# Delta-rule attention and hash-routed experts: the second expert's weights loaded after the last rows, the first expert's last column planned with the attention

## The chip, the core and the metric

The kernel runs on one NeuronCore of a Trainium2 chip. Its engines work side by side, each through its own stream of instructions: TensorE (PE; its weight loads are shown as PEld), VectorE (DVE), ScalarE (ACT), GpSimd (POOL) and SyncE (SP). In this kernel SP issues nearly all transfers, in program order, and POOL issues the scatters of rows. The metric is the device time of one execution in microseconds (us); the kernel before takes 522.31 us, the median of three runs (517.66, 522.31 and 524.82).

## The reference

A delta-rule attention of 4 batches, 8 heads, 768 tokens and a head size of 48 feeds a mixture of 8 experts. A hash of the token's id picks one expert for each token.

```python
k_n = k / (np.linalg.norm(k, axis=-1, keepdims=True) + 1e-06)
for t in range(S):
    y[:, :, t] = np.einsum('bhd,bhde->bhe', q[:, :, t], state)
    v_old = np.einsum('bhde,bhd->bhe', state, kt)
    state = state + bt[:, :, :, None] * np.einsum('bhd,bhe->bhde', kt, vt - v_old)
...
expert_idx = token_ids * np.int64(2654435761) % np.int64(E)
for e in range(E):
    mask = expert_idx == e
    h = np.maximum(xe @ w1[e], 0.0)
    out[mask] = h @ w2[e]
```

The bridge makes 3072 rows of 384 numbers out of the attention's answer. w1 is 384 x 1024 and w2 is 1024 x 384 for each expert, all in float32.

## The kernel before

**Attention.** The 768 tokens are cut into 24 chunks of 32. A chunk asks the state for its values and its answers (`ask`, L631, into psX and psY), solves for its updates (`solve`, L681), adds them to the state (`update`, L704, into psS; the new state is copied out at L727 by ACT and L729 by DVE) and completes the answer (`answer`, L744). The last four chunks (`split`, from `TAIL`) do this in halves, with psX and z1. When a chunk is done, ACT writes its answer to x_sb (L753), and POOL scatters 128 rows to the scratch x_dram, sorted by expert (`store`, L759). DVE computes the triangular inverses and the routing beside it.

**The order** of this part is not written out by hand. Each piece of work is a `task` with an engine, a planned duration, the names it reads and writes, and for matmuls a PSUM bank (`new_job`, `bank`); `order()` plays all tasks through by their planned times and fixes the order on each engine. Tasks marked `idle=True, boost=-1e5` fill PE's idle time or come after the attention. `homes` lists the eight PSUM banks: two z, psX, psY and four psS.

**Experts.** Experts stand in the order `RANKS = [4, 0, 1, 2, 3, 5, 6, 7]`, numbered by how many rows they have. Number 4 is the first expert, number 0 the second, number 1 the third. Each has its own number of rows (up to 424). `gemm1` (L1158) makes the hidden layer in 8 blocks of 128, with the relu on ACT (L1161) and DVE (L1163) in turn; `gemm2_turned` (L1195) or `gemm2` (L1174) gives the result. `send` turns results back (L1205), `store` copies them (L1180), and POOL scatters them to the output (`send_rows`, L1184).

**The first expert** is worked on ahead. Its weights are loaded during the attention into space that is free by then (`weights`, L93 and L959). 18 of the 24 chunks (`SOON`) are enough to hold its first 256 rows (`SC = 2` columns of 128). `early_rows` fetches them to xq0, DVE transposes them (`turn_x`, L107), and `first_expert` adds tasks for both matmuls (L995 and L1006), with the relu at L1000 and the result copied at L1011. Its third column can hold rows of the last chunks. It comes after the attention: `fetch(FIRST)` loads it to xq_late, `turn` transposes it, and `gemm1` and `gemm2` do 128 rows in the first pass of the loop over `RANKS`, in the phase of the experts.

**The second expert's weights** are cut into 8 parts of 384 KB (`load_w_parts`: four of w1 at L93, four of w2 at L124). SP issues three parts after each of the stores that follow the last inverse, so between the last chunks. The third expert's weights are asked for in the first pass of the loop (`between`, `to = i + 2`); x_dram rows of the second are fetched behind those of xq_late, with xq1 as their target.

**PSUM.** The attention's pool `ps` closes at the end of the attention, and three pools open for the experts: `ps_h` with 4 banks for hidden blocks, `ps_t` with 2 for turned results, `ps_o` with 2 for outputs.

## Time and profile before

| what | us |
|---|---|
| the profiled execution's own time | 521.84 |
| its span in the trace | 520.2 |
| median of three runs | 522.31 |
| PE busy in the span | 472.5 (91%) |
| DVE busy | 230.9 (44%) |
| ACT busy | 189.5 (36%) |
| POOL busy | 70.2 (13%) |
| last matmul of the attention ends, by PE's timeline | 247.03 |
| PE begins the second expert | 280.18 |
| last copy of a result begins | 508.18 |

The page gives the busy time of each engine, a picture of the span in 40 slices of 13 us, the queues of the DMA, and the costliest groups of instructions. PEclk is the clock that was granted to PE, in tenths of the full one. In lists of work a line reads: start, duration, engine, line of the kernel, operation, output from input, shapes, how many, and in brackets how long the engine stood idle before and what ended it. "issue" there is idle time in which the engine waited for nothing that the profile shows. SPq is SP's own queue of issued transfers. Large matmuls of float32 leave two records each. A table of stretches gives, for each, the busy time of every engine with its number of records, the granted clock, the DMA's share of busy time (it can go a little above 1) and the rate in GB/s.

### The profile page before, as it was taken

Reading aid. Unit: us, or ns where it says so; the run is one execution under the profiler, and the core shown is the slowest. Engines: PE = TensorE matmul, PEld = TensorE weight load, DVE = VectorE, ACT = ScalarE, POOL = GpSimd, SP = SyncE. Lnnn points to the kernel's source line nnn. Section 1 sums busy time; section 2 is a strip of 40 time slices with the busy share of each in tenths; the row PEclk is TensorE's granted clock in tenths of the full one; section 3 lists DMA queues with packets and bytes.
Section 4 is the critical chain, followed back from the end, with each engine's and each line's share of the span. In section 5 each row is a group of like instructions: output and inputs, shape, how many; then the busy total and the mean of one; then the engine's idle time right before and its main releaser. Section 6 shows DMA issues by size and latency. Waiting matters only on the chain. (4 is left out here: it accounts for less than half of the span.)

```text
span 520.2 us, 15841 instructions
## 1 busy us (share of the span) xinstructions
PE 472.5 (91%) x6652; PEld 322.1 (62%) x6652; DVE 230.9 (44%) x736; ACT 189.5 (36%) x415; POOL 70.2 (13%) x106
## 2 busy tenths in 40 slices
PE   8865999899998888879989999999999999999990
PEld 6654667676776666768766555556555565655650
DVE  5786899899897888643012202103012020120100
ACT  4633687888787677513111101101011020110100
POOL 6000011201102021101010001302202012102010
PEclk9977799999999989968999999999999999999996
DMA  9969758564566274690399954544843006401000
GB/s 145 167 99 139 140 106 148 123 127 90 141 148 129 64 196 92 143 228 34 85 249 203 235 117 129 113 98 137 185 149 82 0 24 159 150 0 41 3 29 15
DMA packets 136748, 60.61 MB, mean 117 GB/s; under 512 B 122957, under 2 KB 131265, under 8 KB 136676
## 3 DMA queue, kind: packets, MB, share of 16 engines
q1 hardware_dynamic: 131140, 49.80, 47.6%
q0 software_dynamic: 5344, 9.66, 5.8%
q8 instruction: 53, 0.87, 0.7%
q10 hardware_dynamic: 192, 0.12, 0.2%
q14 instruction: 19, 0.16, 0.1%
HBM read 49.19 MB, written 10.42 MB: 115 GB/s over the span
## 5 line engine op out<-in xcount | busy, mean ns | idle before, releaser
L1158 PE MATMUL h_ps<-xT,w_sb 128*128 128x424 f32 (+3 forms) x336 | 113.4, 491 | 0.0
L1158 PEld LDWEIGHTS h_ps<-xT,w_sb 128*128 128x128 f32 x336 | 62.9, 190 | 43.1 <-issue 14.9
L1163 DVE TENSOR_SCALAR h_sb<-h_ps 128x424 f32<-128x424 f32 (+4 forms) x32 | 17.0, 531 | 138.7 <-PE h_ps L1158 102.8
L1195 PE MATMUL oT_ps<-h_sb,w_sb 128*128 128x424 f32 (+1 forms) x192 | 66.4, 506 | 0.0
L596 DVE TENSOR_TENSOR tmp<-U,Ni 128x112 f32<-128x112 f32 (+15 forms) x186 | 61.6, 338 | 2.8 <-ACT U L580 0.2
L594 DVE TENSOR_TENSOR U<-U,tmp 128x112 f32<-128x112 f32 (+15 forms) x186 | 61.5, 337 | 2.9
L1184 POOL DMA_INDIRECT out_dram<-o_sb,tokens x26 | 30.3, 1167 | 208.0 <-ACT o_sb L1180 163.0
L1195 PEld LDWEIGHTS oT_ps<-h_sb,w_sb 128*128 128x128 f32 x192 | 36.2, 190 | 28.4 <-issue 15.6
L759 POOL DMA_INDIRECT x_scratch<-x_sb,slot x24 | 24.3, 1011 | 207.5 <-ACT MT L522 123.5
L727 ACT ACTIVATE S<-psS 48x384 f32<-48x384 f32 (+1 forms) x92 | 42.7, 465 | 14.8 <-PE psS L704 13.4
L1174 PE MATMUL o_ps<-w_sb,h_sb 128*121 128x384 f32 (+1 forms) x144 | 46.9, 486 | 0.0
L1161 ACT ACTIVATE h_sb<-h_ps 128x424 f32<-128x424 f32 (+4 forms) x32 | 15.0, 469 | 72.5 <-PE h_ps L1158 72.5
L1174 PEld LDWEIGHTS o_ps<-w_sb,h_sb 128*121 128x121 f32 (+1 forms) x144 | 26.6, 185 | 19.4
L744 PEld LDWEIGHTS psY<-W,MT 64*64 64x64 f32 x768 | 27.0, 144 | 14.0 <-issue 12.4
L704 PE MATMUL psS<-W,K 32*128 32x96 f32 x736 | 28.6, 288 | 5.4 <-ACT W L696 4.7
L744 PE MATMUL psY<-W,MT 64*64 64x48 f32 x768 | 30.8, 230 | 3.0 <-issue 3.0
L1180 ACT COPY o_sb<-o_ps 106x384 f32<-106x384 f32 (+4 forms) x15 | 7.2, 479 | 69.5 <-PE o_ps L1174 55.1
L681 PE MATMUL psX<-R,Tz 64*64 64x48 f32 x672 | 27.9, 223 | 3.5 <-issue 2.5
L704 PEld LDWEIGHTS psS<-W,K 32*128 32x128 f32 x736 | 24.3, 191 | 9.4 <-ACT W L696 7.1
L1197 ACT COPY oT<-oT_ps 128x424 f32<-128x424 f32 (+1 forms) x8 | 4.0, 499 | 70.9 <-PE oT_ps L1195 70.9
L681 PEld LDWEIGHTS psX<-R,Tz 64*64 64x64 f32 x672 | 23.6, 136 | 8.5 <-issue 5.3
L522 ACT ACTIVATE Tz<-TU,kmask 128x256 f32<-128x256 f32 x40 | 25.0, 724 | 0.5 <-DVE TU L610 0.5
(192 smaller groups left out, 586.2 us busy)
## 6 DMA issues: line engine op xcount, KB each, us to landing
w_sb<-in_moe_w_dram SPq DMA_DIRECT2D x32, 384.0 KB
w_sb<-in_moe_w_dram SPq DMA_DIRECT2D x6, 1536.0 KB
keys<-in_k_dram SPq DMA_DIRECT2D x24, 192.0 KB
Qt<-in_q_dram SPq DMA_DIRECT2D x24, 192.0 KB
V<-in_v_dram SPq DMA_DIRECT2D x96, 48.0 KB
K<-in_k_dram SPq DMA_DIRECT2D x96, 48.0 KB
wide<-in_moe_w_dram SPq DMA_DIRECT2D x8, 384.0 KB
xq<-x_scratch SPq DMA_DIRECT2D x12, 144.0 KB
```

Source lines behind the costliest of these rows:

```text
L522: lambda e=e: nc.scalar.activation(out[:, :, e].rearrange(order_of), in_.rearrange(order_of), ACT.Copy, scale=kmask[:, e:e + 1]))
L594: nc.vector.tensor_tensor(U[:, n:, 0:n], U[:, n:, 0:n], t, op=ALU.add)
L596: nc.vector.tensor_tensor(t, U[:, j:n, 0:n].to_broadcast([P, m, n]), Ni[:, j, n:, None].to_broadcast([P, m, n]), op=ALU.mult)
L681: nc.tensor.matmul(pws[i][rows, h], lhsT=Tz[rows, h].rearrange("p e i -> p (e i)"), rhs=R[rows, h], start=(h == (hs.start if split else 0) ...
L704: nc.tensor.matmul(psS[:, b, 2 * D * u:2 * D * u + 2 * D], lhsT=K4[quarter(b), u].rearrange("p r d -> p (r d)"), rhs=W[quarter(b), 2 * u:2 ...
L727: copy = nc.scalar.activation(put, get, ACT.Copy)
L744: nc.tensor.matmul(py[rows, h], lhsT=MT[rows, h].rearrange("p e i -> p (e i)"), rhs=W[rows, h], start=(c == 0 and h == 0), stop=True, skip ...
L759: put = nc.gpsimd.indirect_dma_start(out=x_dram[0:N, :], out_offset=bass.IndirectOffsetOnAxis(ap=slot[:, c:c + 1], axis=0), in_=x_sb, in_o ...
L1158: nc.tensor.matmul(h_ps[:, :width], lhsT=w1_sb[:, co, fo * P:(fo + 1) * P], rhs=xT[:, co, :width], start=(co == 0), stop=(co == CO - 1))
L1174: nc.tensor.matmul(o_ps[0:rows], lhsT=h_sb[:, fo, col * rows:(col + 1) * rows], rhs=w2_sb[:, fo, :], start=(fo == 0), stop=(fo == FO - 1))
L1184: scat = nc.gpsimd.indirect_dma_start(out=out[:, :], out_offset=bass.IndirectOffsetOnAxis(ap=idx, axis=0), in_=rows, in_offset=None, bound ...
L1195: nc.tensor.matmul(oT_ps[:, 0:width], lhsT=w2_sb[:, fo, i * P:(i + 1) * P], rhs=h_sb[:, fo, 0:width], start=(fo == 0), stop=(fo == FO - 1))
```

## The change

Three things are done.

1. The parts of the second expert's weights are no longer issued between the last stores. They follow on SP behind the rows of the late column and the rows of the second expert; the third expert's weights and rows follow them.
2. The first expert's last column becomes a set of tasks, planned with the others. `early_rows` and `number_of` are made general for this (`rows_of`, `columns`). Its input xT_late and its result share a new tile `late`; its hidden layer is kept in xq0; all its relus are ACT's. The loop over `RANKS` skips the first expert.
3. The pool `ps` stays open for the whole program. `hidden()` gives the four banks z0, z1, psX and psY in turn to hidden blocks, and `results()` the four of psS to turned results and outputs alike. xq1 moves from the first pool to a pool of the expert phase, `m_q`.

```diff
-    xqs = [keep.tile([P, NBL, QW], F32, name=f"xq{i}") for i in range(2)]
+    xqs = [keep.tile([P, NBL, QW], F32, name="xq0")]
     xq_late = keep.tile([P, P // C, QW], F32, name="xq_late")
+    late = keep.tile([P, DIN], F32, name="late")
...
+    xT_late, o_late = late.rearrange("p (co x) -> p co x", co=CO), late
+    h_late = xqs[0].rearrange("p i x -> p (i x)")[:, 0:F].rearrange("p (fo x) -> p fo x", fo=FO)
...
-        ps = phase1.enter_context(tc.tile_pool(name="ps", bufs=1, space=PSUM))
+        ps = ctx.enter_context(tc.tile_pool(name="ps", bufs=1, space=PSUM))
...
+            def rows_of(at, cols, xq, numbers):
+                row = value(at, mybir.EngineType.SP, N)
+                got = load_x(row, cols * P // C, xq, nc.sync)
+                got.append(load_numbers(row, cols, P, numbers[:, :, None], nc.sync))
...
+            def columns(name, at, ks, chunks, xq, xq_name, xT):
+                n = ks.stop - ks.start
+                task("SP", 2500, ("x_pad", "lim", *(f"x_dram{i}" for i in range(chunks))),
+                     (xq_name, "numbers" + name),
+                     lambda: rows_of(at, n, xq, numbers_first[:, ks]), kb=200 * n)
+                for c in range(CO):
+                    task("DVE", 70 + 130 * n, (xq_name,), (f"xT{name}{c}",),
+                         lambda c=c: turn_x(xq, n * P // C, xT, c))
+                task("DVE", 220, ("numbers" + name, "lim"), ("idx" + name,),
+                     lambda: number_of(ks))
+
+            columns("", AT_ROW + E + 1, slice(0, SC), SOON, xqs[0], "xq0", xT_first)
...
+            columns("late", AT_ROW + E, slice(SC, SC + 1), NU, xq_late, "xq_late", xT_late)
+            for fo in range(FO):
+                job = new_job(1, early=True)
+                for co in range(CO):
+                    task("PE", 240, ("w1", f"xTlate{co}"), (f"j{job}",),
...
+                         words=2, job=(job, 0), idle=True, boost=-1e5)
+                task("ACT", 290, (f"j{job}",), ("xq0", f"hlate{fo}"), lambda fo=fo, job=job:
+                     nc.scalar.activation(h_late[:, fo], bank(job)[:, 0:P], ACT.Relu),
+                     job=(job, 0))
+            job = new_job(1, early=True)
+            for fo in range(FO):
+                task("PE", 660, ("w2", f"hlate{fo}"), (f"j{job}",),
...
+            task("ACT", 490, (f"j{job}",), tuple(f"xTlate{c}" for c in range(CO)), lambda job=job:
+                 nc.scalar.activation(o_late, bank(job)[:, 0:DIN], ACT.Copy), job=(job, 0))
...
-                if i in stores and parts:
-                    for part in parts[:3]:
-                        part()
-                    parts = parts[3:]
-            for part in parts:
-                part()
-            w_tiles[0] = w1_first, w2_first
...
-         tc.tile_pool(name="m_t", bufs=2) as m_t, \
-         tc.tile_pool(name="ps_h", bufs=4, space=PSUM) as ps_h, \
-         tc.tile_pool(name="ps_t", bufs=2, space=PSUM) as ps_t, \
-         tc.tile_pool(name="ps_o", bufs=2, space=PSUM) as ps_o:
+         tc.tile_pool(name="m_q", bufs=1) as m_q, \
+         tc.tile_pool(name="m_t", bufs=2) as m_t:
+
+        xqs.append(m_q.tile([P, NBL, QW], F32, name="xq1"))
+        banks = itertools.count(), itertools.count()
+
+        def hidden():
+            return homes[next(banks[0]) % 4]
+
+        def results():
+            return homes[4 + next(banks[1]) % 4]
...
         with tc.manual_schedule():
-            fetch(FIRST)
             fetch(RANKS[1])
+            for part in parts:
+                part()
+            w_tiles[2] = load_w(expert_at(RANKS[2], mybir.EngineType.SP), w_pool2, nc.sync)
+            fetch(RANKS[2])
             n_ov = nc.values_load(ov_i[0:1, NOV:NOV + 1], min_val=0, max_val=NOV)
             for c in range(CO):
-                turn(FIRST, c)
+                turn(RANKS[1], c)
             for k in range(SC):
                 send_rows(o_first[:, k], idx_i[:, k:k + 1], True)
+            send_rows(o_late, idx_i[:, SC:SC + 1], True)
             for i, e in enumerate(RANKS):
+                if e == FIRST:
+                    continue
...
-                    to = i + 2 if i < 2 else i + 1
+                    to = max(3, i + 1)
```

More of the change, by code (lines that the diff above doesn't have):

```diff
@@ L140 @@
     h_first = keys.rearrange("p (fo x) -> p fo x", fo=FO)
-    idx_i = keep.tile([P, SC], I32)
-    numbers_first = wide[1][:, FO * DIN + SC * DIN:FO * DIN + SC * DIN + SC]
+    xT_late, o_late = late.rearrange("p (co x) -> p co x", co=CO), late
+    h_late = xqs[0].rearrange("p i x -> p (i x)")[:, 0:F].rearrange("p (fo x) -> p fo x", fo=FO)
+    idx_i = keep.tile([P, SC + 1], I32)
+    numbers_first = wide[1][:, FO * DIN + SC * DIN:FO * DIN + SC * DIN + SC + 1]
     with ExitStack() as phase1:
@@ L970, in first_expert, with number_of @@
                 out=rows, in_=xqs[0].rearrange("p i x -> p (i x)")), kb=700, hold=120000)
-            def early_rows():
-                row = value(AT_ROW + E + 1, mybir.EngineType.SP, N)
-                got = load_x(row, SC * P // C, xqs[0], nc.sync)
-                got.append(load_numbers(row, SC, P, numbers_first[:, :, None], nc.sync))
+            def rows_of(at, cols, xq, numbers):
+                row = value(at, mybir.EngineType.SP, N)
+                got = load_x(row, cols * P // C, xq, nc.sync)
+                got.append(load_numbers(row, cols, P, numbers[:, :, None], nc.sync))
                 for g in got:
                     tc.add_to_no_dep_group("rows", g.ins)
-            task("SP", 2500, ("x_pad", "lim", *(f"x_dram{i}" for i in range(SOON))),
-                 ("xq0", "numbers"), early_rows, kb=400)
-            for c in range(CO):
-                task("DVE", 330, ("xq0",), (f"xT{c}",),
-                     lambda c=c: turn_x(xqs[0], SC * P // C, xT_first, c))
-            def number_of():
-                nc.vector.tensor_tensor(numbers_first, numbers_first,
-                                        none_f[:, FIRST * KT:FIRST * KT + SC], op=ALU.max)
-                nc.vector.tensor_copy(idx_i, numbers_first)
-            task("DVE", 220, ("numbers", "lim"), ("idx",), number_of)
+            def number_of(ks):
+                f = numbers_first[:, ks]
+                nc.vector.tensor_tensor(f, f, none_f[:, FIRST * KT:FIRST * KT + KT][:, ks],
+                                        op=ALU.max)
+                nc.vector.tensor_copy(idx_i[:, ks], f)
+            def columns(name, at, ks, chunks, xq, xq_name, xT):
[9 more added lines that the diff above has]
+            columns("", AT_ROW + E + 1, slice(0, SC), SOON, xqs[0], "xq0", xT_first)
             for fo in range(FO):
@@ L1012, in first_expert @@
                      job=(job, 0))
+            columns("late", AT_ROW + E, slice(SC, SC + 1), NU, xq_late, "xq_late", xT_late)
[3 more added lines that the diff above has]
+                    task("PE", 240, ("w1", f"xTlate{co}"), (f"j{job}",),
+                         lambda fo=fo, co=co, job=job: nc.tensor.matmul(
+                             bank(job)[:, 0:P], lhsT=w1_first[:, co, fo * P:(fo + 1) * P],
+                             rhs=xT_late[:, co], start=(co == 0), stop=(co == CO - 1)),
+                         words=2, job=(job, 0), idle=True, boost=-1e5)
[5 more added lines that the diff above has]
+                task("PE", 660, ("w2", f"hlate{fo}"), (f"j{job}",),
+                     lambda fo=fo, job=job: nc.tensor.matmul(
+                         bank(job)[:, 0:DIN], lhsT=h_late[:, fo], rhs=w2_first[:, fo],
+                         start=(fo == 0), stop=(fo == FO - 1)),
+                     words=2, job=(job, 0), idle=True, boost=-1e5)
+            task("ACT", 490, (f"j{job}",), tuple(f"xTlate{c}" for c in range(CO)), lambda job=job:
+                 nc.scalar.activation(o_late, bank(job)[:, 0:DIN], ACT.Copy), job=(job, 0))
         def note():
@@ L1155, in gemm1 @@
             for fo in range(FO):
-                h_ps = ps_h.tile([P, CAP], F32, name="h_ps")
+                h_ps = hidden()
                 for co in range(CO):
@@ L1171, in gemm2 @@
         def gemm2(w2_sb, h_sb, col, rows, idx, alone):
-            o_ps = ps_o.tile([P, DIN], F32, name="o_ps")
+            o_ps = results()
             for fo in range(FO):
-                nc.tensor.matmul(o_ps[0:rows], lhsT=h_sb[:, fo, col * rows:(col + 1) * rows],
+                nc.tensor.matmul(o_ps[0:rows, 0:DIN], lhsT=h_sb[:, fo, col * rows:(col + 1) * rows],
                                  rhs=w2_sb[:, fo, :], start=(fo == 0), stop=(fo == FO - 1))
@@ L1179, in store @@
             o_sb = o_tiles[next(turns) % len(o_tiles)]
-            (nc.vector.tensor_copy if col % 2 else nc.scalar.copy)(o_sb[0:rows], o_ps[0:rows])
+            (nc.vector.tensor_copy if col % 2 else nc.scalar.copy)(o_sb[0:rows], o_ps[0:rows, 0:DIN])
             send_rows(o_sb[0:rows], idx, alone)
@@ L1191, in gemm2_turned @@
         def gemm2_turned(w2_sb, h_sb, oT, i, width):
-            oT_ps = ps_t.tile([P, CAP], F32, name="oT_ps")
+            oT_ps = results()
             for fo in range(FO):
@@ L1200, in send @@
         def send(oT, e, col):
-            o_ps = ps_o.tile([P, DIN], F32, name="o_ps")
+            o_ps = results()
             cw = CWS[e]
@@ L1212, in own @@
         def own(e):
-            cols, cw = (1, P) if e == FIRST else (KTS[e], CWS[e])
-            xq = xq_late if e == FIRST else xqs[RANKS.index(e) % 2]
-            return cols, cw, (cols * cw + C - 1) // C, xq
+            return KTS[e], CWS[e], (CAPS[e] + C - 1) // C, xqs[RANKS.index(e) % 2]
         def fetch(e):
             cols, cw, blocks, xq = own(e)
-            row = value(AT_ROW + (E if e == FIRST else e), mybir.EngineType.SP, N)
+            row = value(AT_ROW + e, mybir.EngineType.SP, N)
             load_x(row, blocks, xq, nc.sync)
@@ L1229, in turn @@
             if c == CO - 1:
-                at = e * KT + (SC if e == FIRST else 0)
+                at = e * KT
                 f = xns.pop(e)[0:cw, 0:cols]
@@ L1236 @@
         with tc.manual_schedule():
-            fetch(FIRST)
             fetch(RANKS[1])
+            for part in parts:
+                part()
+            w_tiles[2] = load_w(expert_at(RANKS[2], mybir.EngineType.SP), w_pool2, nc.sync)
+            fetch(RANKS[2])
             n_ov = nc.values_load(ov_i[0:1, NOV:NOV + 1], min_val=0, max_val=NOV)
             for c in range(CO):
-                turn(FIRST, c)
+                turn(RANKS[1], c)
             for k in range(SC):
                 send_rows(o_first[:, k], idx_i[:, k:k + 1], True)
+            send_rows(o_late, idx_i[:, SC:SC + 1], True)
             for i, e in enumerate(RANKS):
+                if e == FIRST:
+                    continue
                 w1_sb, w2_sb = w_tiles.pop(i)
                 rest = [e for e in RANKS[i + 1:i + 3]]
-                done = RANKS[i - 1] if i and RANKS[i - 1] in oTs else None
+                done = RANKS[i - 1] if RANKS[i - 1] in oTs else None
                 def between(fo):
-                    to = i + 2 if i < 2 else i + 1
+                    to = max(3, i + 1)
                     if fo == 0 and to < E and to not in w_tiles:
@@ L1262 @@
                 h_sb = m_h.tile([P, FO, CAP], F32, name="h_sb")
-                gemm1(w1_sb, xTs.pop(e), h_sb, CAPS[e] if i else P, between)
+                gemm1(w1_sb, xTs.pop(e), h_sb, CAPS[e], between)
                 if KTS[e] > CO:
```

## The prediction

> **What bounds the kernel now.** I read the page first: the share of each engine, then the slices. The chain that ended last says nothing here (its whole length is POOL's last scatter), so I went on to the waits and the timeline of PE, which is busy 91% of the span.

> ```profile
> span 520.2 us, 15841 instructions
> PE 472.5 (91%) x6652; PEld 322.1 (62%) x6652; DVE 230.9 (44%) x736; ACT 189.5 (36%) x415; POOL 70.2 (13%) x106
> ...
> PEclk9977799999999989968999999999999999999996
> ```

> The PEclk row has a hole at slice 18, about 221 to 234 us. By the timeline, PE's attention part ends at 247.03 us. From there PE is busy without a break to 508.9 us, but for two short waits; these are all that the waits of PE list for 247 to 509 us:

> ```profile
> PE h_ps L1158 <- ACT wide L1011: 1.0, 1, 1.0
> PE psS L1006 <- ACT keys L1000: 0.5, 1, 0.5
> ```

> So after 247 us time is matmul work, and the change leaves that work alone. Time can be won only in those 1.43 us (0.96 and 0.47 in the timeline) and before 247 us. There PE's timeline, and below it the table by stretches of 2 us (PE, PEld, DVE, ACT and POOL busy; granted clock; DMA share; GB/s), show this:

> ```profile
> 221.81 0.49 PE L744 MATMUL psY<-W,MT 64*64 64x48 f32 x9
> 225.27 1.52 PE L744 MATMUL psY<-W,MT 64*64 64x48 f32 x23 [2.98 <-issue]
> ```
> ```profile
> 222.00:224.00 2.00, 0.29 (x9) 0.23 (x7) 1.53 (x5) 1.30 (x4) 0.00 (x0) 1.00 1.27 206
> 224.00:226.00 2.00, 0.73 (x15) 0.72 (x16) 0.00 (x0) 0.00 (x0) 0.00 (x0) 0.70 1.04 213
> 226.00:228.00 2.00, 2.00 (x46) 1.91 (x46) 0.97 (x2) 0.49 (x1) 0.00 (x0) 0.50 1.04 359
> ...
> 236.00:238.00 2.00, 2.00 (x34) 1.35 (x37) 0.94 (x2) 0.62 (x2) 0.57 (x1) 0.50 0.00 0
> 238.00:240.00 2.00, 2.00 (x67) 1.79 (x60) 0.71 (x2) 0.08 (x1) 0.60 (x2) 0.89 0.30 111
> ```

> PE stops for 2.98 us after 9 of 32 equal matmul records, where no semaphore stands, and then runs at half clock to about 238.5 us. The stop falls where the DMA share has been 0.97 to 1.27 since 216 us. What SP issued there is the second expert's weights:

> ```profile
> 215.13 1.35 SPq L93 DMA_DIRECT2D w_sb<-in_moe_w_dram  x3
> ...
> 218.70 0.33 SPq L93 DMA_DIRECT2D w_sb<-in_moe_w_dram  x1
> 219.63 2.18 SPq L124 DMA_DIRECT2D w_sb<-in_moe_w_dram  x2
> ...
> 227.32 1.20 SPq L124 DMA_DIRECT2D w_sb<-in_moe_w_dram  x2
> ```

> I take the stop for PE waiting for its own instructions. Such stops in mid-run recur about once a chunk: with DMA at a share of 0.3 to 0.8 they last 0.20 to 0.21 us (199.85, 206.67 and 213.48 us), and one more long one (2.05 us at 161.24) came while the first expert's L93 weights filled the DMA at 1.05 to 1.30.

> **Part 1: the weights go behind the last rows.** Removed from 215 to 228 us: 8 transfers of 384 KB. The last chunks' K loads, which stood between them in SP's queue, come sooner. Chunk by chunk, from the first question (L631, psX) to the next one:
> - Chunk 20 takes 9.99 us (216.73 to 226.72). Without the stop its 23 remaining matmuls take 23/32 of 1.06 us (the spacing of such a run at 209.51), to 223.07. Next in line is the first half of the new state, ready when two of DVE's four L729 copies are done, at 223.18. The question starts at about 223.25: 3.5 us saved.
> - Chunk 21 takes 10.01 us at half clock. From rows at full clock: first question to first solve 2.15 (0.47, a wait for the last state copy to 0.75, 0.47, then 0.93 for the two L631 on psY), solve to update 1.10 (239.20 to 240.30), the two updates and two answers 0.55 + 0.53 + 0.55 + 0.53, one early matmul 0.43; sum 5.84, and the state copy is ready at the same time, say 5.9. Saved: 4.1.
> - Chunk 22 takes 5.73, by the same rows 2.15 + 1.10 + 1.10 + 1.06 = 5.4. Saved: 0.3. Chunk 23 is at full clock already.

> That is 7.9 us, less two short stops of 0.2 that stay: **7.5 us**. Bounds: if the stop goes and the clock falls all the same, 2.8; if chunks 21 and 22 each fell to the 4.57 us of chunk 23, 3.5 + 5.4 + 1.2 = 10.1; if the stop has another cause, 0. I take the sum from rows of the same split chunks.

> [...]

> Where the transfers land now: by the built order of the changed kernel, SP issues the last rows (xq_late), the rows of expert 0 (xq1), the 8 parts, the weights of expert 1, and then its rows. With T the end of attention (247.03 now), xq_late waits for the last scatter and is issued at T+4.3, xq1 at T+7.6, the parts from T+10.6. Price of transfers: from 262 to 276 us the DMA moved one expert's 3.15 MB and 0.69 MB of rows in 14 us. So 0.69 + 3.15 MB end at about T+25, w1's half at T+19. The first expert ends at T+33.15 now: 14 us of cover. The next 3.15 MB end near T+37, and expert 1 starts at about T+67. Cost nothing.

> New wait: xq0 is also the late column's hidden layer, so SP's fetch of expert 1's rows waits for PE's last late matmul, about T+33. Behind it on SP stand expert 2's weights (due near T+102) and rows. Lands at about T+40. The DVE transposes are due at T+37.5 and stand ahead of the relus of blocks 3, 5 and 7 on DVE; PE needs the first of these at its block 7, T+33 + 7 x 2.13 = T+48. Cover 8 us, cost nothing.

> **Part 2: the late column among the tasks.** The same 24 matmuls of 128 columns (48 records, 5.46 us) and 8 of 384 (16 records, 5.16), now between the first expert's. PE reaches the first of them after 17 matmuls of 0.43 and 8 of 0.645, at T+12.5 or later; its input is ready at T+8.6 (255.63 now). No wait. Moved to ACT: 4 relus that DVE did, 0.28 us each, ACT being almost idle there. SP's two register loads for it (0.28 us each) run while SP waits for the last scatter anyway, and POOL's third output scatter stays third. The two old waits go (1.43 us). But in the built order PE follows its own relu closely at three places: matmul drain 0.2 + relu 0.28 to 0.38 + 0.06, less the matmuls between, gives 0.54, 0.51 and, at the last matmul, 0.66. Sum 1.71: **+0.3 us**. Bounds -1.4 and +1.5 (another place of each kind).

> **Part 3: PSUM banks in one set.** The 0.96 us was the change of pools; it is counted above. Later, 4 banks serve the hidden blocks as before; the other 4 serve two uses that had 2 each. Each use is emptied by a copy of about 0.5 us, the next one is 4.6 us off: nothing. No bank was waited for before; if one were in each of six experts, at 0.5 us, +3.

> DVE's order in chunks 8 to 17 also shifts (scale_v earlier, routing later, by some 1.5 us). No wait of PE from 100 to 215 us names these: 0, with 1 us to either side.

> **Sum**, against the profiled execution's 521.84 us (520.2 and 1.64 around it): 521.84 - 7.5 + 0.3 = **514.6 us**. That execution is 0.47 under the median of 522.31, so the ratio to it is about 0.985. About 2% is what a measurement of this kernel can tell from no change (its three runs span 1.4%).

> **Rivals.**
> - Half the gain: the stop is gone or shortened, but PE's gaps still let the clock fall, or another long stop comes elsewhere. For: after a stretch with PE busy 1.01 of 2 us (184 to 186 us) the clock fell to 0.50 although no long stop was there. Against: chunks 20 to 23 are busier. 521.8 - 2.8 = 519, or 517 to 520.5. Chance 0.18.
> - The change misses its mark: the stop isn't from the weights. For: the trace names no cause. Against: the two longest mid-run stops after 100 us both stand in weight loads. 522, 520.5 to 523.5. Chance 0.08.
> - Larger gain: tail chunks at chunk 23's pace and no new relu waits: 521.8 - 10.1 - 1.4 = 510.3, range 509 to 512. Chance 0.10.
> - **Slower:** the waiting fetch of expert 1's rows is late. A full queue makes four such issues take 8.39 us (262.98) and 8.96 (280.95) instead of 1.9; issued at T+33 behind unfinished weights, rows land at T+45 or after. From T+48 each us late stands on PE, and from T+56 the whole gain is eaten: 523 to 535. Needs twice the queueing seen. Chance 0.05.
> - The forecast, 512 to 517: 0.59.

> The range leaves out the ends of the last four: 509.5 to 520.5. Faster by over 2% (below 511.9): the larger gain, and 0.14 for an error in the chunks' sum or the runs' spread, 0.24. Slower by over 2% (above 532.8): the far end of the late rows, 0.03. Within: 0.73.

> **What would show it.** Right: no PE stop over 1 us between 200 us and the end of attention; granted clock 1.00 there; attention's end near 239.5; PE's first expert-0 matmul 33 to 34 us later. Part 2 is wrong if the three short PE waits on ACT are absent or if PE waits for DVE at the first late matmul. The forecast is wrong if the clock still shows 0.50 before attention's end, if the stop reappears, or if PE waits for w_sb, xT or h_sb early in expert 0.

## The result

The changed kernel is slower: 538.00 us, median of four executions (536.64 to 540.54), against 523.57 of the kernel before (517.66 to 525.08). The ratio is 1.0303, 95% interval 1.0211 to 1.0395. The prediction was 514.6 us.

The page of the changed kernel (span and engines, the clock of PE in 40 slices, two groups of matmuls with their busy time and the idle time ahead of them):

```profile
span 536.9 us, 15851 instructions
...
PE 481.1 (90%) x6652; PEld 321.6 (60%) x6652; DVE 229.9 (43%) x732; ACT 190.6 (35%) x419; POOL 70.4 (13%) x106
...
PEclk9967999999995799999999999999999999999996
...
L1227 PE MATMUL psS<-h_sb,w_sb 128*128 128x424 f32 (+1 forms) x192 | 68.9, 512 | 7.7 <-DVE oT L1229 3.0
...
L1206 PE MATMUL psS<-w_sb,h_sb 128*121 128x384 f32 (+1 forms) x144 | 48.6, 491 | 4.6 <-DVE o_sb L1212 2.2
```

The hole of the clock at slice 18 is gone, as predicted, and another stands at slices 13 and 14 (161 to 188 us). The two groups of result matmuls (7.7 and 4.6 us of idle time) now wait for DVE and ACT. Cut at the same events, the two profiled executions differ so:

| stretch | before | after | difference |
|---|---|---|---|
| to the first question of chunk 20 | 216.73 | 222.11 | +5.4 |
| from there to the end of attention | 30.30 | 23.23 | -7.1 |
| to the second expert's first matmul | 33.15 | 34.30 | +1.15 |
| second to last expert on PE (to 508.10; 524.80) | 227.92 | 245.16 | +17.24 |
| what comes behind PE | 12.1 | 12.1 | 0 |
| span | 520.2 | 536.9 | +16.7 |

**Where the 17 us are.** In the kernel before, PE ran without a break here. These are all waits of PE from 279 us on in the changed kernel (line waited for: us in total, times, longest):

```profile
PE psS L1227 <- DVE oT L1229: 3.0, 4, 0.8
PE psS L1227 <- DVE o_sb L1212: 2.4, 3, 0.8
PE psS L1227 <- ACT oT L1229: 2.4, 4, 0.6
PE psS L1206 <- DVE o_sb L1212: 2.2, 3, 0.8
PE psS L1206 <- ACT o_sb L1212: 1.7, 3, 0.6
PE psS L1206 <- DVEq L1309: 0.7, 1, 0.7
PE z L1190 <- issue: 0.4, 1, 0.4
```

The first six lines are 18 waits for a copy, 12.4 us. PE's timeline shows some in their place; first the turned results of the second expert before, then after:

```profile
297.26 17.24 PE L1195 MATMUL oT_ps<-h_sb,w_sb 128*128 128x424 f32 x48
314.34 4.43 PE L1158 MATMUL h_ps<-xT,w_sb 128*128 128x424 f32 x12
```
```profile
296.80 5.86 PE L1227 MATMUL psS<-h_sb,w_sb 128*128 128x424 f32 x16
303.25 5.96 PE L1227 MATMUL psS<-h_sb,w_sb 128*128 128x424 f32 x16 [0.60 <-ACT oT L1229]
309.98 5.96 PE L1227 MATMUL psS<-h_sb,w_sb 128*128 128x424 f32 x16 [0.76 <-DVE oT L1229]
315.77 4.43 PE L1190 MATMUL z<-xT,w_sb 128*128 128x424 f32 x12
...
333.84 0.49 PE L1237 MATMUL psS<-ident,oT 128*106 128x128 f32 x3
335.16 5.96 PE L1227 MATMUL psS<-h_sb,w_sb 128*128 128x424 f32 x16 [0.83 <-DVE o_sb L1212]
```

The second set of 16 matmul records waits for the copy of the first set, the third for the copy of the second, although `results()` hands each a different bank. A set takes 17.24 / 3 = 5.75 us when nothing waits; from set to set it is now 6.5 to 6.7. A wait costs some 0.2 us more than its idle time (0.60, 0.76 and 0.83 us, where the spacing below gives 0.81, 0.97 and 0.99); where that goes isn't shown. Taken from the spacing of the sets, it is 0.81 us behind an ACT copy (341.72 - 335.16 - 5.75), 0.97 behind a DVE copy (348.44 - 341.72 - 5.75), 0.99 behind a turned output (335.16 - 333.84, where the next work came 0.33 us after the transposes before). Seven experts have the first two, four of them the third: 7 x (0.81 + 0.97) + 4 x 0.99 = **16.4 us**, an estimate, since each price is read from one place.

The table leaves these theories. **One tile:** psS is allocated as a single tile of four banks (`psS = ps.tile([P, B, BANK])`, `homes` are slices of it), so a matmul into one of its banks is made to wait for the last copy out of any of them. **Rivals:** the four banks come round too soon now that two uses share them; or the loss is in late weights or in the clock.

### The profile page after: what moved, and what is told of

It is laid out like the page before. It is cut to its first block, busy times and chain, and to the rows that moved or that the text cites. A ratio compares the mean times of both kernels' runs of the same rounds, so it can differ in the third digit from the quotient of the medians.

```text
span 536.9 us, 15851 instructions
## 1 busy us (share of the span) xinstructions
PE 481.1 (90%) x6652; PEld 321.6 (60%) x6652; DVE 229.9 (43%) x732; ACT 190.6 (35%) x419; POOL 70.4 (13%) x106
## 5 line engine op out<-in xcount | busy, mean ns | idle before, releaser
L1227 PE MATMUL psS<-h_sb,w_sb 128*128 128x424 f32 (+1 forms) x192 | 68.9, 512 | 7.7 <-DVE oT L1229 3.0
L1227 PEld LDWEIGHTS psS<-h_sb,w_sb 128*128 128x128 f32 x192 | 35.6, 190 | 39.7 <-issue 14.3
L1190 PE MATMUL z<-xT,w_sb 128*128 128x424 f32 (+3 forms) x168 | 57.5, 492 | 0.4 <-issue 0.4
L1206 PE MATMUL psS<-w_sb,h_sb 128*121 128x384 f32 (+1 forms) x144 | 48.6, 491 | 4.6 <-DVE o_sb L1212 2.2
L1195 DVE TENSOR_SCALAR h_sb<-z 128x424 f32<-128x424 f32 (+3 forms) x14 | 7.9, 565 | 98.2 <-PE z L1190 98.2
L1190 PEld LDWEIGHTS z<-xT,w_sb 128*128 128x128 f32 x168 | 31.5, 190 | 22.9 <-issue 8.6
L1206 PEld LDWEIGHTS psS<-w_sb,h_sb 128*121 128x121 f32 (+1 forms) x144 | 26.1, 185 | 26.4 <-DVE o_sb L1212 3.7
L748 PEld LDWEIGHTS psY<-W,MT 64*64 64x64 f32 x768 | 25.5, 138 | 12.1 <-issue 10.6
L1212 ACT COPY o_sb<-psS 106x384 f32<-106x384 f32 (+3 forms) x14 | 6.7, 479 | 70.4 <-PE psS L1206 56.0
L1190 PE MATMUL psX<-xT,w_sb 128*128 128x424 f32 (+3 forms) x84 | 29.9, 492 | 0.0
L1190 PE MATMUL psY<-xT,w_sb 128*128 128x424 f32 (+3 forms) x84 | 29.9, 491 | 0.0
```

What stands on the lines that cost most here:

```text
L748: nc.tensor.matmul(py[rows, h], lhsT=MT[rows, h].rearrange("p e i -> p (e i)"), rhs=W[rows, h], start=(c == 0 and h == 0), stop=True, skip ...
L1190: nc.tensor.matmul(h_ps[:, :width], lhsT=w1_sb[:, co, fo * P:(fo + 1) * P], rhs=xT[:, co, :width], start=(co == 0), stop=(co == CO - 1))
L1195: nc.vector.tensor_scalar(out=h_sb[:, fo, :width], in0=h_ps[:, :width], scalar1=0.0, scalar2=None, op0=ALU.max)
L1206: nc.tensor.matmul(o_ps[0:rows, 0:DIN], lhsT=h_sb[:, fo, col * rows:(col + 1) * rows], rhs=w2_sb[:, fo, :], start=(fo == 0), stop=(fo == F ...
L1227: nc.tensor.matmul(oT_ps[:, 0:width], lhsT=w2_sb[:, fo, i * P:(i + 1) * P], rhs=h_sb[:, fo, 0:width], start=(fo == 0), stop=(fo == FO - 1))
```

## The experiments

Kernels run together share executions of the kernel before on the same chip, and chips differ: its median beside the kernels below was 523.08 us (four_tiles, own_pools, behind_only, one_set_only), 522.82 (behind_four, spread, before_again, swapped) and 517.65 (best, spread_turns, late_only, one_by_one). Across these groups ratios are compared. A median is of 4 or 10 executions, or of one where that is said.

### Half as many banks, each its own tile

```diff
         def hidden():
-            return homes[next(banks[0]) % 4]
+            return homes[next(banks[0]) % 2]
         def results():
-            return homes[4 + next(banks[1]) % 4]
+            return homes[2 + next(banks[1]) % 2]
```

> The changed kernel with half as many PSUM banks in the expert phase: hidden blocks take z0 and z1 in turn, results take psX and psY; the four banks of psS, which are one tile, are not used there. Theory 'one tile': a matmul into any bank of psS waits for the copy out of whichever bank of psS was filled before it, because the four banks are one tile. In the trace that is 18 waits, which cost 0.81 us (behind an ACT copy), 0.97 (behind a DVE copy) or 0.99 (behind the copy of a turned output) in the spacing of the matmuls: 7 x (0.81 + 0.97) + 4 x 0.99 = 16.4 us. They all go: 538.5 - 16.4 = 522 us, no wait of PE for a copy after the second expert's start. Rival 'too few banks' (two uses share banks that one use had before, and come round too soon): half the banks make it worse, 540 us or more. Rival 'loads or clock' (the loss is in late weights or in the clock): 538 us, unchanged.

Measured: 521.69 us, ratio to before 0.9959 (0.9925 to 0.9993). All 18 waits are gone with half the banks. Two others came: 0.4 us for weights at the second expert's first matmul, and this one, of which more below:

```profile
PE z L1190 <- DVE h_sb L1195: 1.8, 1, 1.8
```

"Too few banks" is out for the results, and so is "loads or clock": parts 1 and 2 are still in this kernel.

### Part 3 undone, and part 3 alone

`own_pools` is the changed kernel with the three pools of before (ps_h, ps_t, ps_o); `one_set_only` is the kernel before with this:

```diff
-        ps = phase1.enter_context(tc.tile_pool(name="ps", bufs=1, space=PSUM))
+        ps = ctx.enter_context(tc.tile_pool(name="ps", bufs=1, space=PSUM))
...
-                h_ps = ps_h.tile([P, CAP], F32, name="h_ps")
+                h_ps = hidden()
...
-            oT_ps = ps_t.tile([P, CAP], F32, name="oT_ps")
+            oT_ps = results()
...
-            o_ps = ps_o.tile([P, DIN], F32, name="o_ps")
+            o_ps = results()
```

> The changed kernel with part 3 undone: the attention's PSUM pool closes, and three pools open for the experts, with a tile for each bank, as in the kernel before. 'One tile': the 16.4 us go and the wait at the change of pools (0.96 us before) comes back: 538.5 - 16.4 + 1 = 523 us. 'Too few banks': the same, 522 to 523. 'Loads or clock': 538 us, since parts 1 and 2 are in it.

> The kernel before with part 3 alone: one set of PSUM banks for the whole program, hidden blocks on z0, z1, psX and psY, results on the four banks of psS. 'One tile': the 16.4 us appear here by themselves, less the 0.96 us of the change of pools, and 2 x about 0.9 more at most for the late column's result: 521.8 + 16.4 - 1.0 = 537 us, up to 539. 'Loads or clock': 521 us.

Measured: `own_pools` 522.59 us, 0.9989 (0.9952 to 1.0027); `one_set_only` 539.45 us, 1.0299 (1.0228 to 1.0370), 16.4 us over the 523.08 of before. PE's waits in the expert phase of `one_set_only` are those of the changed kernel, line for line, with the same counts and sums; the first two:

```profile
PE psS L1200 <- DVE oT L1202: 3.0, 4, 0.8
PE psS L1200 <- DVE o_sb L1185: 2.4, 3, 0.8
```

Part 3 alone makes the loss, and taking it out returns it. A rival that no expectation named is that psS's banks themselves are slower to hand over. The programs that `before` and `own_pools` build rule it out: their result tiles lie on the same four banks (4 to 7), one tile to a bank, and PE waits for none of them. It is the tile, not the banks. A declared independence of the banks, as `renew` has it, was not tried.

### The sets exchanged: a larger dose

```diff
-            return homes[next(banks[0]) % 4]
+            return homes[4 + next(banks[0]) % 4]
...
-            return homes[4 + next(banks[1]) % 4]
+            return homes[next(banks[1]) % 4]
```

> The changed kernel with the two sets of banks exchanged: hidden blocks on the four banks of psS, results on z0, z1, psX and psY. 'One tile': the 18 waits behind results go (16.4 us), and every hidden block but the first of each of seven experts now waits for the relu of the block before it, 49 waits of 0.8 to 1.0 us: 538.5 - 16.4 + 44 = 566 us (560 to 572), with waits of PE psS for h_sb on ACT and DVE in turn. Rival 'too few banks for results' (results of two uses share four banks): 538 us, since each set still has four.

Measured: 567.13 us (one execution). The waits of PE behind relus, and one of them in the timeline:

```profile
PE psS L1190 <- ACT h_sb L1193: 16.5, 28, 0.7
PE psS L1190 <- DVE h_sb L1195: 11.8, 21, 0.8
```
```profile
287.12 2.40 PE L1190 MATMUL psS<-xT,w_sb 128*128 128x424 f32 x6 [0.74 <-ACT h_sb L1193]
290.29 2.40 PE L1190 MATMUL psS<-xT,w_sb 128*128 128x424 f32 x6 [0.76 <-DVE h_sb L1195]
```

28 + 21 = 49 waits, as counted ahead, with four banks in each set as in the changed kernel. Blocks that took 2.13 us now start about 3.1 us apart. Three doses (no use of psS in the phase of the experts, results on it, hidden blocks on it) gave 522, 538 and 567 us: the tile is the cause.

### Part 1 alone

```diff
-                if i in stores and parts:
-                    for part in parts[:3]:
-                        part()
-                    parts = parts[3:]
-            for part in parts:
-                part()
...
             fetch(FIRST)
             fetch(RANKS[1])
+            for part in parts:
+                part()
```

> The kernel before with part 1 alone: the second expert's weights are issued behind the rows of the late column and of the second expert. The planned order of the attention is that of before. If the prediction's first step holds by itself: 521.8 - 7.5 = 514 us, attention's end near 239.5 us, no stop of PE over 1 us after 200 us. If the stop and the half clock come earlier whatever stands in the tail (in the changed kernel chunks 10 and 11 lost 5.4 us at half clock from 162 to 182 us): 519 to 520 us, attention's end at 245. If the weights now come too late for the second expert: a wait of PE for w_sb before its first matmul, and no gain.

Measured: 519.13 us, 4.0 under the 523.08 of before; the ratio of the comparison is 0.9959 (0.9917 to 1.0001), so 2 us by the ratio (0 to 4.3) and 4 by the medians, not 7.5. Yet its profile has the predicted tail: 23.25 us from chunk 20's first question to the end of attention, no long stop, full clock. What differs is what it is compared with. Before chunk 20, `behind_only` stops for 2.58 us near 160 us and then runs at half clock from 161 to 179 us. The profiled execution of before had that stop too (2.05 us), but the clock held. The same stretch in the kernel before, and then in the changed kernel, whose clock falls there too (2 us each: busy time of the engines, granted clock, DMA share, GB/s):

```profile
160.00:162.00 2.00, 0.76 (x21) 0.67 (x24) 0.34 (x2) 0.48 (x3) 0.00 (x0) 1.00 0.65 130
162.00:164.00 2.00, 2.00 (x43) 1.31 (x38) 1.86 (x5) 1.99 (x4) 0.00 (x0) 1.00 0.35 67
```
```profile
160.00:162.00 2.00, 0.00 (x0) 0.00 (x0) 0.19 (x1) 1.09 (x3) 0.00 (x0) 0.93 0.48 121
162.00:164.00 2.00, 1.95 (x32) 1.78 (x36) 1.34 (x4) 1.08 (x2) 0.00 (x0) 0.50 0.52 98
```

So a second profile of the kernel before was taken.

> The kernel before once more, for a second profile of it. The first profile shows the stop near 161 us (2.05 us) and full clock after it, while the five later profiles of other kernels show half clock for 17 to 20 us after the same stop. If the half clock there is a matter of the single execution: this profile may show it, with the tail's half clock as well or without it, and its time goes with the us of clock that are missing (0.58 us of time for each over the executions of before). If the planned order of before protects it: full clock from 150 to 185 us again.

Measured: 522.55 us (one execution). Its clock, and in PE's timeline the stop near 161 us:

```profile
PEclk9967899999997699979999999999999999999997
```
```profile
161.39 0.30 PE L465 MATMUL z<-KQ 48*32 48x64 f32 x4 [2.60 <-issue]
```

Here the clock falls from 162 to 179 us, and the tail's stop (2.99 us, ending at 228.80) is followed by only 7 us of half clock, to 234, where the first profile had about 14. From chunk 20's first question to the end of attention it takes 220.25 to 247.76, 27.5 us: part 1's 23.25 is 4.3 us better than this execution and 7.05 better than the first. The stops are in both profiles; how long the clock stays down differs between them. The other profiles agree. In the five profiles with weights between the last stores (`before`, `before_again`, `one_set_only`, `late_only`, `one_by_one`) the longest stop between 200 us and the end of attention is 1.81 to 2.99 us, with 7 to 14 us of half clock. In the nine without, it is 0.30 us at most, at full clock. Over the 25 executions of before beside the first four kernels, the mean clock runs from 0.967 (518.00 us) to 0.944 (527.35 us).

### One part of the weights behind each store

```diff
-                    for part in parts[:3]:
+                    for part in parts[:1]:
...
-                    parts = parts[3:]
+                    parts = parts[1:]
```

> The kernel before with one edit: one part of the second expert's weights behind each store of the tail, not three (the parts that are left go out behind the last store). 'Instructions': the stop of 2.98 and 2.99 us near 222 to 229 us in both profiles of before, where three parts are in flight, goes under 1 us, and the tail's half clock with it: 519 us, as with part 1 whole. If any weights in the tail make the stop: a stop over 2 us, 522 to 523 us.

Measured: 515.60 us, 0.9975 (0.9936 to 1.0014): no gain that can be told. In its profile, which is of its slowest execution (521.75 us), the stop in the stretch of the single parts is 0.77 us, where three parts at a time had 2.98 and 2.99; but the six parts that were left went out in a run from 225.7 to 230.6 us, as SP had nothing else left between them, and the long stop comes behind that:

```profile
236.05 0.77 PE L681 MATMUL psX<-R,Tz 64*64 64x48 f32 x9 [2.85 <-issue]
```

Here single parts went with a short stop, a run of parts with a long one. The expectation that all of the tail would be free was wrong, since I had not read where the rest is issued.

### The other run of weights taken apart

`behind_four` is part 1 with four separate tiles as in `four_tiles`, on the kernel before; `spread` puts the four w1 transfers of the first expert at four places of SP's order:

```diff
-            weights(0)
+            HOLDS = (0, 134000, 144000, 168000)
+            for j in range(4):
+                w1_part(j)
...
+                task("SP", 700, ("lim",), (tuple(
+                    f"KQ2{a}{b}" for a in range(2) for b in range(B)) if not j else ()) + ("w1",),
+                     go, kb=150, hold=HOLDS[j])
```

> The kernel before with part 1, and with one set of PSUM banks that are four separate tiles in the expert phase (hidden blocks on z0 and z1, results on psX and psY), late column as before. 'One tile': part 1's time (519.1 us alone) less the 0.96 us at the change of pools: 518 us, and no wait of PE for a copy in the expert phase. If keeping the pool open has a price of its own apart from the tile: 520 us or more.

> The kernel behind_four with the first expert's w1 load taken apart: its four transfers of 384 KB stand at four places of SP's order, with the chunks' K and V loads between them, and not in one run at 149 us. The order on PE and DVE is unchanged. Theory 'instructions': PE's own instructions come by DMA in packets of 16 KB, and the run of weights makes one of them late, so that PE stops for 2.0 to 2.8 us near 161 us in every profile so far; the half clock that follows it in most (17 to 20 us long) costs about 5 us more. Then the stop falls to 0.5 us or less, no half clock follows, and the time is 518 - 2 - 5 = 511 us. Rival 'not from the weights': the stop near 161 us stays over 1.5 us, 518 us. Rival 'only moved': a stop over 1.5 us comes at another place between 150 and 200 us, 515 to 518 us.

Measured: `behind_four` 524.37 us, 1.0034 (0.9997 to 1.0071); `spread` 516.96 us, 0.9884 (0.9822 to 0.9947). Between the two lie 7.4 us, as expected (7), though both stand about 6 us above what was expected. In the profiles the stop of 2.69 us at 162.73 and the half clock from 163 to 180 us are gone; the longest stop without a releaser from 150 to 200 us is 0.95. So the run of weights is behind the long stop near 161 us, and without that stop the long half clock did not come in `spread`. The stop doesn't always bring it: the first profile of the kernel before kept the clock.

What PE waits for there can be narrowed down: the profile of the kernel before lists a DMA queue q8 of the kind "instruction", with 53 packets of 16 KB, one for about every 250 of PE's 13304 instructions and one in every 3 to 10 us of the attention. The DMA view of 0.1 us of the kernel before, from 222.0, has this line; 79.2% of 16 engines for 0.1 us is 1.27 us for the packet:

```profile
q8 instruction: 1, 0.02, 79.2%
```

PE stops 0.3 us after that packet begins and goes on at 225.27, 2.0 us after it ends. All fifteen stops over 2 us in the fourteen profiles after 100 us lie so: they begin between 0.4 us before the start of a packet and 1.1 us after it, and end 1.2 to 2.0 us after its end. The DMA share is 1.01 to 1.24 in the 3 us ahead of the packet and 0.59 to 1.20 in the 3 us behind its start. With a share under 0.6 on both sides, the stops are 0.9 us at most (`spread_turns`), most of them 0.4 or less, though some of those packets take over 1.5 us too.

A busy DMA isn't enough by itself. At the packet at 198.3 in `own_pools` the shares are 1.02 and 1.13 and PE stops for 0.24 us; at the one at 108.6 in the kernel before they are 1.05 and 0.94 and it doesn't stop. The four w2 transfers of the first expert, also in one run near 190 us, brought no stop over 0.3 us. What tells these apart isn't settled. So that the weights bring the long stops is shown by taking them away; that PE lacks instructions then is an inference from the packets. Nor is it shown where the 1.2 us or more go by which each long stop outlasts its packet.

At most of the packets PE stops for 0.4 us or not at all; beside the runs of weights at the places above the stop is 2 to 3 us.

How long the half clock lasts can be read: the traces of the kernel before and of the changed kernel record whole stretches at 0.50 of 3.41, 6.83, 10.24, 13.65 and 20.48 us, each a multiple of 3.413 within 0.01 us, and in `before_again` one of about 17 (162 to 179). What sets their length isn't shown. The stop near 161 us was followed by one in one profile of the kernel before and not in the other, though the stops differ too (2.60 and 2.05 us). A busy PE did not end it: in the changed kernel PE is busy for 1.80 to 2.00 of every 2 us from 162 to 182 us, at 0.50.

### A wait that two hidden banks let through

`behind_four` came 6 us over its expectation, and `spread` with it. In its profile PE waits 3.57 us at the second expert (4.49 in `spread`), and 6.8 us of half clock come with it. In `spread`, DVE and SP's queue:

```profile
282.40 0.65 DVE L107 STREAM_TRANSPOSE xT<-xq 128x448 f32<-128x448 f32 x1 [9.07 <-DMA xq<-x_scratch]
282.96 0.56 DVE L1174 TENSOR_SCALAR h_sb<-z 128x424 f32<-128x424 f32 x1
```
```profile
283.58 9.65 PE L1169 MATMUL z<-xT,w_sb 128*128 128x424 f32 x18 [4.49 <-DVE h_sb L1174]
```
```profile
262.88 11.92 SPq L99 DMA_DIRECT2D xq<-x_scratch  x4
```

This is the prediction's slower rival: the third expert's rows stand behind 6.3 MB of weights, their four issues take 11.92 us instead of 1.9, and DVE's relus stand behind the transposes of those rows. With two hidden banks PE is reached. To tell lateness from the number of banks, the transposes were moved behind later relus:

```diff
-                    if fo % 2 and fo // 2 < CO and rest:
-                        turn(rest[0], fo // 2)
+                    if fo % 2 and fo > 1 and rest:
+                        turn(rest[0], fo // 2 - 1)
```

> The kernel spread with one edit: DVE's three transposes of the next expert's rows stand behind the relus of blocks 3, 5 and 7, not 1, 3 and 5. In spread PE waits 4.49 us at the second expert's fourth block for DVE's relu, which stands behind a transpose that waits 9.07 us for rows; half clock follows for 8 us (3.4 us of clock missing). Theory 'late rows behind part 1': the wait goes to under 0.5 us and the half clock goes with it: 517.0 - 4.5 - 1.7 = 511 us. Rival 'two hidden banks are too few': the wait for the relu stays, 517 us.

Measured: 503.65 us, 0.9733 (0.9675 to 0.9791), with two hidden banks still. The wait is 0.4 us, and no half clock follows in the phase of the experts. By ratio that is 1.5% under `spread`, about 8 us; 6 were expected, and the half clock was mis-sized: in the profile of `spread`, 6.8 us at half clock on a bound PE are 3.4 us of work, not 1.7.

### Part 1 with the other run taken apart, banks as before

The first expert's w1 as in `spread`, on `behind_only`.

> The kernel before with part 1 and with the w1 load of the first expert taken apart as in spread; PSUM pools as before (four banks for hidden blocks). Spread removed the half clock after 161 us and left a stop of 0.95 us: its profile reaches the end of attention 8.2 us before behind_four's (last scatter 238.2 against 246.5). So 519.1 (part 1 alone) less 8 less nothing: 511 us, with no wait of PE behind DVE's relus at the second expert's start, since four banks give two blocks more of cover than the two banks of spread. If the gain of spread was a gain of the single execution: 517 to 519 us.

Measured: 505.51 us, 0.9779 (0.9719 to 0.9838), no wait of PE in the expert phase but the change of pools. A stop of 0.97 us at 163.94 is left, and 3.4 us of half clock with it. Against `behind_only`'s 0.9959 that is 1.8% or 9 us, where 8 were expected. DVE waits 8.10 us for rows here too, and with four hidden banks PE doesn't wait. `best` and `spread_turns` beat both kernels; on 523 us their ratios mean about 511 and 509. Both intervals lie below 1; only that of `spread_turns` lies below 0.98.

### Part 2 alone

The changed kernel with parts 1 and 3 undone.

> The kernel before with part 2 alone: the late column among the tasks, the second expert's weights between the last stores, PSUM pools as before; the third expert's weights are asked for before the first pass. The prediction had +0.3 for part 2: 523 us. Own_pools (parts 1 and 2) is 3.5 us slower than behind_only (part 1), in the profiles by 1.3 us before 75 us and by 2.2 us in chunks 5 to 12, so by the runs so far it should be 524 to 526.5. If the difference between those two was one of executions: 523 or less.

Measured: 519.18 us, 1.0035 (0.9999 to 1.0072), so 0 to 3.8 us, 1.8 in the middle. The prediction's +0.3 is inside, and the 3.5 us between `own_pools` and `behind_only` just so. Which chunks it would cost isn't settled: from one copied answer to the next, chunk 9 takes 9.4 us in the changed kernel (to 140.1) against 8.4 before, 0.77 of it a stop without a releaser at 138.8; but it takes 8.0 in `four_tiles`, which has the same order.

## Why the prediction was wrong

**What bounds the kernel** held: PE's work after the attention, and every wait put into it adds to the end.

**Part 3** is the step that failed: "Each use is emptied by a copy of about 0.5 us, the next one is 4.6 us off: nothing." It counted banks and copies, and took each bank to be waited for by itself. With the banks in one tile, a set waits for the copy of the set before it, 18 times, and the part measures 16.4 us (`one_set_only`). The bound of +3 failed for the same reason, and no rival held this mechanism; the slower one named late rows. The code told it: psS is one tile, z0, z1, psX and psY are four, and `renew` takes copies out of psS apart by hand with the reason "other banks, other places". The trace of before could not show it in the expert phase, where each bank had its own tile. Just ahead of that phase it did: of the two waits that the prediction printed, the second (0.47 us, L1006 behind the relu of L1000) is, in the built program, a matmul on hidden block 6 into one bank of psS that is held for the relu of block 7 out of another.

**Part 1:** the mechanism was right. The stop is gone, the clock full from 200 us to the end of attention, the tail 7.1 us shorter in the profile (7.5 predicted). The mis-sized term is what that is worth over many executions: 2 to 4 us. The sum took the first profile's 14 us of half clock as the kernel's, where a second profile of the same kernel has 7; among five profiles with weights there, the tail takes 27.5 to 30.3 us, and the first is the longest. Even the shortest is 4.3 us over the 23.25 of `behind_only`, so why the ratio gives 2 is in part open. The rival of half the gain has 519, and part 1 alone measured 519.1, which is luck in part: that rival takes the stop elsewhere for one that the change brings, and the kernel before had it too. Attention ended at 245.34, not near 239.5, because chunks 12 and 13 (10 and 11 in the expectation of `behind_only`) ran at half clock behind the stop near 161 us, 7.3 us longer than before; the later chunks won 2.5 back. The prediction had that stop in its hands ("one more long one (2.05 us at 161.24)") and used it only as evidence of the cause.

**The late rows** came later than T+40: they landed at 290.4, 45 us behind the end of attention. DVE's relu of block 3 was done at 291.6, and PE's block 7, which takes its bank, began at 294.66. The cover was 8 us on paper and 3 in the run.

```profile
290.45 0.65 DVE L108 STREAM_TRANSPOSE xT<-xq 128x448 f32<-128x448 f32 x1 [5.60 <-DMA xq<-x_scratch]
291.02 0.56 DVE L1195 TENSOR_SCALAR h_sb<-psY 128x424 f32<-128x424 f32 x1
...
294.66 2.30 PE L1190 MATMUL psY<-xT,w_sb 128*128 128x424 f32 x6
```

**Part 2:** the late column is at its place without a wait for its input. The three short waits on ACT appear, 0.42, 0.37 and 0.58 us in idle time where 0.54, 0.51 and 0.66 were the full price, and a fourth stop of 0.42 us before the second expert. The stretch is +1.15 us, inside the bounds of -1.4 and +1.5. The reason given was wrong: "PE follows its own relu closely" describes none of the three. Two of its terms stand in rows of before: a relu of L1000 begins 0.20 us after PE has gone on to the next matmul (its 0.2; 260.37 to 260.57), and PE goes on 0.06 us after the copy that it waits for (269.50 to 269.56).

```profile
259.95 0.49 PE L1029 MATMUL psS<-late,wide 128*128 128x128 f32 x2 [0.42 <-ACT xq L1034]
274.88 0.91 PE L1016 MATMUL psS<-wide,keys 128*128 128x384 f32 x2 [0.37 <-ACT xq L1034]
278.31 0.91 PE L1039 MATMUL psS<-wide,xq 128*128 128x384 f32 x2 [0.58 <-ACT wide L1021]
```

Neither L1029 nor L1016 reads xq, which the late column's relu writes; the third wait is for the copy of a result. In the built program all three matmuls write one bank of psS while ACT reads another: the same false wait, inside the planned tasks. The built order that the prediction read for part 2 had the mechanism that part 3 put at nothing.

Multiplied, the ratios of the three parts alone give 0.9959 x 1.0035 x 1.0299 = 1.029; the whole change measured 1.030. The parts explain it.

## What to carry to other kernels

Before banks or buffers are put into one pool, look at how they are allocated: work on slices of one tile can wait for its neighbours. Here the price was 0.8 to 1.0 us at every use, with four banks in the tile. A stop "issue" in mid-run next to a run of large transfers is worth moving (7.4 us between `behind_four` and `spread`, 2 to 4 us in `behind_only`), but its price has to come from more than one execution where the clock falls with it. A load that is moved to where there is cover pushes back what is queued behind it (here rows landed 45 us behind the end of attention, where 40 were counted); count the cover of that too.
